# First V in three pieces with the first w_in pieces between them, and four FFN banks filled by head pairs

## The chip, the cores and the metric

The kernel runs on one core of a Trainium2 chip. The metric is device time of one execution in microseconds (us); every run is checked against the reference. A change counts as faster or slower from 2% on. The span that a profile shows is some 1.8 us shorter than the time of the same execution (before: 510.0 against 511.74). Every run quoted here is compared with runs of the same rounds. Some traces lack a few matmul records (before: 2710 matmuls but 2761 weight loads); where one is missing, the view shows a short idle time put down to "issue".

## The reference

Linformer attention, then a squared-ReLU feed-forward network (FFN), all in float32 outside the kernel:

```python
# q, k, v: (8 batches, 8 heads, 1024 tokens, 64);  E, F: (64, 1024)
k_proj = einsum('ks,bhsd->bhkd', E, k);  v_proj = einsum('ks,bhsd->bhkd', F, v)
attn = softmax(q @ k_proj.T / 8)                    # 64 columns
x = (attn @ v_proj) -> (8192 tokens, 512)
out = relu(x @ w_in) ** 2 @ w_out                   # 512 -> 2048 -> 512
```

The FFN is nearly all of the TensorE work. Each later batch's attention is spread among the FFN matmuls of the batch before. The first batch has nothing to hide behind, so the first 25 us or so, the head, are where TensorE can idle. The change is to the head alone.

## The kernel before

The program loads float32 and converts to bfloat16 on the way, on one queue issued by GpSimd (`load`). The loads of the head, in order: K and Q of the first batch by halves, V by halves, then w_in in five pieces and w_out in four:

```python
    for g in range(2):
        load(K0[:, half[g]], tokens(k, 0, h=half[g]))
        load(Q0[:, half[g], 0:4, :], tokens(q, 0, h=half[g], i=slice(0, 4)))
        if g == 0:
            make_identity(nc, ident[:])
            load(f_bf[:], F[:])
    for g in range(2):
        load(V0[:, half[g]], tokens(v, 0, h=half[g]))
```

```python
    W_IN_PIECES = ((0, 2), (2, 4), (4, 8), (8, 12), (12, 16))
    w_in_view = moe_w_in.rearrange("(cb p) f -> p cb f", p=P)
    w_out_view = moe_w_out.rearrange("(fb p) m -> p fb m", p=P)
    w_in_at, w_out_sb = {}, []
    for lo, hi in W_IN_PIECES:
        t = wpool.tile([P, NCB, (hi - lo) * P], BF16, name=f"w_in_{lo}")
        load(t[:], w_in_view[:, :, lo * P:hi * P])
        for fb in range(lo, hi):
            w_in_at[fb] = (t, fb - lo)
    fn = NFB // WP
    for j in range(WP):
        if j == WP - 1:
            load(Q0[:, :, 4:8, :], tokens(q, 0, i=slice(4, 8)))
        t = wpool.tile([P, fn, DM], BF16, name=f"w_out_{j}")
        load(t[:], w_out_view[:, j * fn:(j + 1) * fn, :])
        w_out_sb.append(t)
```

V is projected by F (1024 tokens to 64), half the heads at a time, into both halves of the partitions; `chunk_values` multiplies the exponentials with that and scales the result by the inverse sums into `xT`, the FFN's input. One call covers a group of two head pairs, which are two of xT's four channel blocks:

```python
        def project_v(self, g):

            ps = bank()
            for i in range(NI):
                for o in (LO, HI):
                    nc.tensor.matmul(
                        ps[o, 0:C // 2], lhsT=FT[:, i, :], rhs=V0[:, half[g], i, :],
                        start=(i == 0), stop=(i == NI - 1),
                    )
            nc.vector.tensor_copy(self.vp[:, half[g]], ps[:, 0:C // 2].rearrange("k (h d) -> k h d", d=D))
```

```python
        def chunk_values(self, c, g):
            ps = att_psum()
            e, rs = self.e.pop(g), self.rs.pop(g)
            for j in range(2):
                s = slice(j * HC, (j + 1) * HC)
                self.values_mm(ps[:, :, s], 2 * g + j, e[:, :, s])
            for j in range(2):
                s = slice(j * HC, (j + 1) * HC)
                nc.vector.tensor_tensor(
                    out=self.xT[:, 2 * g + j, c], in0=ps[:, :, s], in1=rs[:, :, s], op=ALU.mult
                )
```

The FFN's first token half starts in two banks of PSUM, the memory that TensorE writes its results to: channel blocks 0 and 1 (head group 0), then 2 and 3 (group 1). Then 14 more banks, then w_out's four pieces in order, for two token blocks at a time:

```python
        def steps(self):
            for c in range(2):
                self.hsq[c] = hsq_pool.tile([P, NFB, TCH], BF16, name="hsq")
                first = self.cold and c == 0
                fb0 = 0
                if first:

                    banks = [bank() for _ in range(2)]
                    for g in range(2):
                        for fb in range(2):
                            for cb in (2 * g, 2 * g + 1):
                                self.first_mm(c, fb, cb, banks[fb])
                            if g == 1:
                                self.square(c, fb, banks[fb])
                        yield
                    fb0 = 2
                for fb in range(fb0, NFB):
                    ps = bank()
                    for cb in range(NCB):
                        self.first_mm(c, fb, cb, ps)
                    self.square(c, fb, ps)
                    yield
                if first:

                    for t0 in range(0, 4, 2):
                        banks = [bank() for _ in range(2)]
                        for j in range(WP):
                            for t in range(2):
                                for fb in range(j * fn, (j + 1) * fn):
                                    self.second_mm(c, t0 + t, fb, banks[t])
                                if j == WP - 1:
                                    self.store(c, t0 + t, banks[t])
                                yield
```

(cut: the ordinary second half.) TensorE's order is written by hand; `warm(n)` issues n matmuls on zeros that only keep the array busy. The end of the head, before the FFN loop:

```python
        att.transpose_k((1,))
        warm(2)
        att.chunk_scores(0, 1)
        warm(2)
        att.project_v(0)
        warm(1)
        att.chunk_sums(0, 1)
        att.chunk_values(0, 0)
        warm(1)
        att.project_v(1)
        att.chunk_values(0, 1)
```

The softmax here doesn't subtract the row's maximum and nothing guards it: scores larger than these inputs give would overflow.

## Time and profile before

| before | |
|---|---|
| time | 512.42 us (511.70 to 512.67, 3 runs) |
| span of the profiled run | 510.0 us |
| TensorE busy | 497.0 us, 97% |
| first V projection begins | 15.98 us |
| FFN reaches the third w_in piece | 25.57 us |
| matmuls of the last w_out piece begin | 42.35 us |

The first extract is TensorE's timeline of the kernel before. Columns: start, duration, engine, line, operation, output<-inputs, shapes, count; in brackets the idle time before it and what ended that.

```profile
15.98 1.06 PE L204 MATMUL ps_bank<-V_sb,FT 128*64 128x256 bf16 x16
17.30 0.41 PE L262 MATMUL ps_att<-expT,ones 64*64 64x512 bf16 x4 [0.25 <-issue]
...
19.74 1.06 PE L204 MATMUL ps_bank<-V_sb,FT 128*64 128x256 bf16 x16 [1.44 <-DMA V_sb<-in_v_dram]
21.32 0.41 PE L266 MATMUL ps_att<-expT,vp 64*64 64x256 bf16 x8 [0.52 <-DVE vp L208]
21.67 1.31 PE L358 MATMUL ps_bank<-xT,w_in_114 128*128 128x512 bf16 x5
23.19 0.81 PE L358 MATMUL ps_bank<-xT,w_in_114 128*128 128x512 bf16 x3 [0.22 <-DVE xT L341]
...
25.57 3.62 PE L358 MATMUL ps_bank<-xT,w_in_118 128*128 128x512 bf16 x16
...
42.35 1.02 PE L364 MATMUL ps_bank<-w_out_131,hsq 128*128 128x512 bf16 x4 [0.19 <-DMA w_out_131<-in_moe_w_out_dram]
```

The reader should see the 1.44 us wait for V's second half, the 0.52 us wait for its cast, and the third w_in piece at 25.57. These are the waits that the change is about. (A busy time ends with the modelled drain of the array; back to back, matmuls of 512 columns follow each other every 0.216 us.)

The second is the chain of waits of the kernel before, in order of time: start, duration, what.

```profile
7.67 14.18 DMA w_in_116<-in_moe_w_in_dram
...
22.14 20.17 DMA w_out_131<-in_moe_w_out_dram
...
42.35 1.04 PE ps_bank L364 x4
```

The chain does not pass through V at all. It runs through the landing of the second w_in piece, which frees a slot in the load queue, and then through the landing of the last w_out piece at 42.31 (issued at 22.14, 20.17 us to landing).

The third is the table of stages of the kernel before: from:to and length, busy time of PE, PEld, DVE, ACT and POOL with counts, granted clock, DMA share, GB/s.

```profile
15.00:20.00 5.00, 3.26 (x45) 1.77 (x48) 1.72 (x3) 3.67 (x4) 0.76 (x2) 1.00 1.33 201
20.00:25.00 5.00, 4.26 (x37) 2.03 (x33) 2.41 (x5) 1.18 (x3) 2.65 (x4) 1.00 1.26 206
25.00:30.00 5.00, 4.95 (x24) 2.26 (x24) 2.43 (x7) 3.48 (x6) 1.69 (x3) 1.00 1.24 206
```

The loads run at a level 201 to 206 GB/s. TensorE is busy 3.26 of 5 us in the stage with the wait for V, and nearly all the time from 25 on.

The last is GpSimd's timeline of the kernel before: its two issues of w_out pieces that were released by the landings of V's two halves.

```profile
16.22 0.74 POOL L76 DMA_DIRECT2D w_out_126<-in_moe_w_out_dram  x1 [1.83 <-DMA V_sb<-in_v_dram]
19.98 0.74 POOL L76 DMA_DIRECT2D w_out_128<-in_moe_w_out_dram  x1 [3.02 <-DMA V_sb<-in_v_dram]
```

The halves, 512 KB each, landed 3.76 us apart in this trace.

### The profile page before, as it was taken

Reading aid. Unit: us, or ns where it says so; the run is one execution under the profiler, and the core shown is the slowest. Engines: PE = TensorE matmul, PEld = TensorE weight load, DVE = VectorE, ACT = ScalarE, POOL = GpSimd, SP = SyncE. Lnnn points to the kernel's source line nnn. Section 1 sums busy time; section 2 is a strip of 40 time slices with the busy share of each in tenths; the row PEclk is TensorE's granted clock in tenths of the full one; section 3 lists DMA queues with packets and bytes.
Section 4 is the critical chain, followed back from the end, with each engine's and each line's share of the span. In section 5 each row is a group of like instructions: output and inputs, shape, how many; then the busy total and the mean of one; then the engine's idle time right before and its main releaser. Section 6 shows DMA issues by size and latency. Waiting matters only on the chain.

```text
span 510.0 us, 6889 instructions
## 1 busy us (share of the span) xinstructions
PE 497.0 (97%) x2710; PEld 222.8 (44%) x2761; DVE 216.7 (42%) x437; ACT 272.4 (53%) x411; POOL 32.0 (6%) x44
## 2 busy tenths in 40 slices
PE   8799999999999999999999999999999999999997
PEld 4344444444444444444444444444444444444444
DVE  2442766444434445235452345444443443522130
ACT  2564484664718556374645736366472755544351
POOL 7320100121000020001000000000000000000000
PEclk9999999999999999999999999999999999999999
DMA  9999999899996199104931060101102011010102
GB/s 156 204 205 222 226 207 202 132 220 207 195 217 125 56 185 201 65 0 126 181 78 42 17 160 1 62 22 42 53 1 82 1 41 42 31 54 21 63 0 82
DMA packets 67840, 53.92 MB, mean 106 GB/s; under 512 B 29152, under 2 KB 59616, under 8 KB 67808
## 3 DMA queue, kind: packets, MB, share of 16 engines
q0 software_dynamic: 30880, 29.49, 36.8%
q1 hardware_dynamic: 36928, 23.99, 17.5%
q8 instruction: 21, 0.34, 0.3%
q14 instruction: 11, 0.09, 0.1%
HBM read 59.24 MB, written 16.78 MB: 149 GB/s over the span
## 4 chain that ended last, share of the span: by engine, by line
PE 88%; DMA 7%; issue 2%; POOL 1%; ACT 1%; DVE 1%; POOLq 0%; ACTq 0%
PE ps_bank L364 41%; PE ps_bank L358 40%; DMA w_out_131<-in_moe_w_out_dram 4%; DMA w_in_116<-in_moe_w_in_dram 3%; PE ps_bank L185 2%; PE ps_att L256 1%; PE ps_att L290 1%; PE ps_att L312 1%; PE ps_bank L312 1%; DVE rs L300 0%; PE ps_bank L241 0%; DVE xT L341 0%; POOL K_sb L76 0%; POOL V_sb L76 0%; ACT expT L270 0%
## 5 line engine op out<-in xcount | busy, mean ns | idle before, releaser
L355 DVE TENSOR_TENSOR hsq<-h_relu 128x512 bf16<-128x512 bf16 x256 | 108.9, 426 | 192.9 <-ACT h_relu L354 192.0
L354 ACT ACTIVATE h_relu<-ps_bank 128x512 bf16<-128x512 f32 x256 | 151.7, 599 | 69.3 <-PE ps_bank L358 69.2
L364 PEld LDWEIGHTS <-hsq 128*128 128x128 bf16 x1040 | 99.5, 98 | 123.6 <-issue 9.3
L371 ACT COPY o_sb<-ps_bank 128x512 f32<-128x512 f32 (+1 forms) x65 | 37.6, 579 | 119.7 <-PE ps_bank L364 110.9
L364 PE MATMUL ps_bank<-w_out_124,hsq 128*128 128x512 bf16 (+1 forms) x257 | 65.6, 376 | 0.2
L364 PE MATMUL ps_bank<-w_out_131,hsq 128*128 128x512 bf16 (+1 forms) x251 | 64.1, 376 | 1.4 <-issue 1.1
L364 PE MATMUL ps_bank<-w_out_128,hsq 128*128 128x512 bf16 (+1 forms) x252 | 64.3, 376 | 1.1 <-issue 1.0
L364 PE MATMUL ps_bank<-w_out_126,hsq 128*128 128x512 bf16 (+1 forms) x249 | 64.2, 376 | 1.1 <-issue 0.8
L300 DVE COPY rs<-rs 32x1024 f32<-32x1024 f32 x60 | 41.3, 689 | 47.2 <-ACT rs L295 45.8
L358 PE MATMUL ps_bank<-xT,w_in_122 128*128 128x512 bf16 x255 | 58.9, 380 | 0.0
L358 PE MATMUL ps_bank<-xT,w_in_118 128*128 128x512 bf16 x250 | 57.7, 380 | 0.4
L358 PE MATMUL ps_bank<-xT,w_in_120 128*128 128x512 bf16 x247 | 57.4, 379 | 0.4
L270 ACT ACTIVATE expT<-ps_att 128x1024 bf16<-128x1024 f32 x32 | 31.8, 1024 | 18.1 <-PE ps_att L256 18.1
L358 PEld LDWEIGHTS <-w_in_120 128*128 128x128 bf16 x256 | 24.9, 98 | 30.4 <-issue 0.4
L358 PEld LDWEIGHTS <-w_in_118 128*128 128x128 bf16 x256 | 24.9, 98 | 30.2 <-issue 0.4
L358 PEld LDWEIGHTS <-w_in_122 128*128 128x128 bf16 x256 | 24.4, 98 | 31.1 <-issue 2.7
L358 PE MATMUL ps_bank<-xT,w_in_114 128*128 128x512 bf16 x128 | 30.6, 379 | 0.3 <-DVE xT L341 0.2
L358 PE MATMUL ps_bank<-xT,w_in_116 128*128 128x512 bf16 x126 | 30.0, 379 | 0.1
L294 ACT ACTIVATE rs<-ps_att 128x1024 f32<-128x1024 f32 x15 | 15.3, 1023 | 12.7 <-PE ps_att L290 12.7
L316 DVE TENSOR_TENSOR xT<-ps_att,rs 128x512 bf16<-128x512 f32 x28 | 18.1, 686 | 8.7 <-PE ps_att L312 8.4
L358 PEld LDWEIGHTS <-w_in_114 128*128 128x128 bf16 x128 | 12.4, 98 | 15.6 <-issue 1.3
L358 PEld LDWEIGHTS <-w_in_116 128*128 128x128 bf16 x128 | 12.5, 98 | 15.2 <-issue 0.2
(71 smaller groups left out, 233.9 us busy)
## 6 DMA issues: line engine op xcount, KB each, us to landing
out_dram<-o_sb SPq DMA_DIRECT2D x63, 256.0 KB, 2.0
K_sb<-in_k_dram POOLq DMA_DIRECT2D x7, 1024.0 KB, 22.1
V_sb<-in_v_dram POOLq DMA_DIRECT2D x7, 1024.0 KB, 26.7
Q_sb<-in_q_dram POOLq DMA_DIRECT2D x7, 1024.0 KB, 15.0
K_sb<-in_k_dram POOLq DMA_DIRECT2D x2, 512.0 KB, 7.1
V_sb<-in_v_dram POOLq DMA_DIRECT2D x2, 512.0 KB, 12.0
Q_sb<-in_q_dram POOLq DMA_DIRECT2D x2, 256.0 KB, 7.6
w_in_118<-in_moe_w_in_dram POOLq DMA_DIRECT2D x1, 512.0 KB, 15.5
```

The costliest lines, as they stand in the source:

```text
L185: nc.tensor.matmul(ps[LO, :], lhsT=ET[:, i, :], rhs=self.K[:, :, i, :], start=f, stop=l)
L256: nc.tensor.matmul(ps[o, par], lhsT=self.kT[r, h % 4, h // 4, :], rhs=self.qT[r, h, n, :], start=True, stop=True)
L270: nc.scalar.activation(e[:], ps[:], AF.Exp, scale=SCALE)
L294: nc.scalar.activation(rs[1][:], ps[:], AF.Ln)
L300: nc.vector.tensor_copy(rs[j][lack:lack + 32], rs[j][have:have + 32])
L312: nc.tensor.matmul(ps_x[par][o], lhsT=self.vp[r, 2 * pr + a, :], rhs=e[r, par], start=True, stop=True)
L316: nc.vector.tensor_tensor(out=self.xT[:, pr, :, par], in0=ps_x[par].rearrange("p (c t) -> p c t", c=2), in1=rs[:, par].rearrange("p (c t) ...
L354: nc.scalar.activation(r[:], ps[:], AF.Relu)
L355: nc.vector.tensor_tensor(out=self.hsq[c][:, fb, :], in0=r[:], in1=r[:], op=ALU.mult)
L358: nc.tensor.matmul(ps[:], lhsT=w_in_blk(cb, fb), rhs=self.xT[:, cb, c].rearrange("p a t -> p (a t)"), start=(cb == 0), stop=(cb == NCB - 1),)
L364: nc.tensor.matmul(ps[:, m], lhsT=self.hsq[c][:, fb, tb * P:(tb + 1) * P], rhs=w_out_blk(fb)[:, m], start=(fb == 0), stop=(fb == NFB - 1),)
L371: nc.scalar.copy(o[:, m], ps[:, m])
```

## The change

The intent: begin the FFN before all of V is there. V comes in pieces of 4, 2 and 2 heads with the first two w_in pieces between them. The FFN starts in four banks instead of two on head group 0, and the last two head pairs of V are projected, multiplied and folded in one after the other while the rest lands.

```diff
--- before.py
+++ after.py
@@ -96,8 +96,8 @@
         if g == 0:
             make_identity(nc, ident[:])
             load(f_bf[:], F[:])
-    for g in range(2):
-        load(V0[:, half[g]], tokens(v, 0, h=half[g]))
+    V_PIECES = (slice(0, 4), slice(4, 6), slice(6, 8))
+    load(V0[:, V_PIECES[0]], tokens(v, 0, h=V_PIECES[0]))
     nc.scalar.preload_act_table_set("natural_log_exp_and_others")
     zeros = const_pool.tile([P, 512], BF16, name="zeros")
     nc.vector.memset(zeros[:], 0.0)
@@ -109,11 +109,13 @@
     w_in_view = moe_w_in.rearrange("(cb p) f -> p cb f", p=P)
     w_out_view = moe_w_out.rearrange("(fb p) m -> p fb m", p=P)
     w_in_at, w_out_sb = {}, []
-    for lo, hi in W_IN_PIECES:
+    for j, (lo, hi) in enumerate(W_IN_PIECES):
         t = wpool.tile([P, NCB, (hi - lo) * P], BF16, name=f"w_in_{lo}")
         load(t[:], w_in_view[:, :, lo * P:hi * P])
         for fb in range(lo, hi):
             w_in_at[fb] = (t, fb - lo)
+        if j < 2:
+            load(V0[:, V_PIECES[j + 1]], tokens(v, 0, h=V_PIECES[j + 1]))
     fn = NFB // WP
     for j in range(WP):
         if j == WP - 1:
@@ -196,16 +198,16 @@
                 )
             self.keep_k(ps[LO, 0:C // 2], g, nc.scalar.copy if g == 0 else None)
 
-        def project_v(self, g):
-
-            ps = bank()
+        def project_v(self, h):
+
+            n = (h.stop - h.start) * D
+            ps = att_psum()[:, 0, 0:n]
             for i in range(NI):
                 for o in (LO, HI):
                     nc.tensor.matmul(
-                        ps[o, 0:C // 2], lhsT=FT[:, i, :], rhs=V0[:, half[g], i, :],
-                        start=(i == 0), stop=(i == NI - 1),
+                        ps[o], lhsT=FT[:, i, :], rhs=V0[:, h, i, :], start=(i == 0), stop=(i == NI - 1)
                     )
-            nc.vector.tensor_copy(self.vp[:, half[g]], ps[:, 0:C // 2].rearrange("k (h d) -> k h d", d=D))
+            nc.vector.tensor_copy(self.vp[:, h], ps.rearrange("k (h d) -> k h d", d=D))
 
         def transpose_k(self, gs=(0, 1)):
             ps = bank([P, H // 2, 2, KP], BF16)
@@ -330,13 +332,13 @@
             self.sums_mm(ps, self.e[g])
             self.rs[g] = self.inverse(ps)
 
-        def chunk_values(self, c, g):
+        def chunk_values(self, c, g, pairs=(0, 1)):
             ps = att_psum()
-            e, rs = self.e.pop(g), self.rs.pop(g)
-            for j in range(2):
+            e, rs = self.e[g], self.rs[g]
+            for j in pairs:
                 s = slice(j * HC, (j + 1) * HC)
                 self.values_mm(ps[:, :, s], 2 * g + j, e[:, :, s])
-            for j in range(2):
+            for j in pairs:
                 s = slice(j * HC, (j + 1) * HC)
                 nc.vector.tensor_tensor(
                     out=self.xT[:, 2 * g + j, c], in0=ps[:, :, s], in1=rs[:, :, s], op=ALU.mult
@@ -379,15 +381,18 @@
                 fb0 = 0
                 if first:
 
-                    banks = [bank() for _ in range(2)]
-                    for g in range(2):
-                        for fb in range(2):
-                            for cb in (2 * g, 2 * g + 1):
+                    banks = [bank() for _ in range(4)]
+                    for cbs, fbs in (
+                        ((0, 1), (0, 1)), ((0, 1), (2, 3)), ((2,), (0, 1)), ((2,), (2, 3)), ((3,), (0, 1, 2, 3)),
+                    ):
+                        for fb in fbs:
+                            for cb in cbs:
                                 self.first_mm(c, fb, cb, banks[fb])
-                            if g == 1:
+                            if cbs[-1] == NCB - 1:
                                 self.square(c, fb, banks[fb])
-                        yield
-                    fb0 = 2
+                        if (cbs, fbs) != ((2,), (2, 3)):
+                            yield
+                    fb0 = 4
                 for fb in range(fb0, NFB):
                     ps = bank()
                     for cb in range(NCB):
@@ -446,13 +451,11 @@
         warm(2)
         att.chunk_scores(0, 1)
         warm(2)
-        att.project_v(0)
+        att.project_v(V_PIECES[0])
         warm(1)
         att.chunk_sums(0, 1)
         att.chunk_values(0, 0)
-        warm(1)
-        att.project_v(1)
-        att.chunk_values(0, 1)
+        warm(2)
 
         coming = None
         for b in range(B):
@@ -462,6 +465,10 @@
                 plan.setdefault(step, []).append(lambda: fn(*args, **kwargs))
 
             if b == 0:
+                at(1, att.project_v, V_PIECES[1])
+                at(2, att.chunk_values, 0, 1, (0,))
+                at(2, att.project_v, V_PIECES[2])
+                at(3, att.chunk_values, 0, 1, (1,))
                 at(21, att.transpose_q_chunk, 1, Q0, 0)
                 at(21, att.transpose_q_chunk, 1, Q0, 1)
                 at(23, att.chunk_scores, 1, 0)
```

On TensorE this is 17 more matmuls (16 narrow projections and one warming); on GpSimd one more load is issued.

## The prediction

> **What bounds the kernel now.** The page gives PE 97% busy at full granted clock in a span of 510.0 us, so only the head of the program has idle TensorE time: in the stage table PE is busy 3.26 of the 5 us from 15 to 20, 4.26 from 20 to 25, and then 4.95 to 5.00. The PE timeline shows the two waits the change aims at: 1.44 us at 18.3-19.7 for the second half of V, and 0.52 us at 20.8-21.3 for the cast of vp, plus 0.22 us for xT; the FFN flows from 23.2 and reaches the third w_in piece at 25.57.
>
> But the chain of waits does not run through these. Its first 43 us are descriptor issues on GpSimd, then the landing of the second w_in piece (issued 7.67, landed 21.85), then that of the last w_out piece (issued 22.14, landed 42.31); PE starts on that piece at 42.35, having waited only 0.19 us. The stage table has the DMA engines at over 1.2 and a level 201 to 207 GB/s from 10 to 43 us. Until 42.3 us the program is DMA-bound: every 512 KB piece lands some 2.55 us after the last (24.4, 26.9, 29.5, 32.0, 34.6, 37.1, 39.8, 42.3), while PE comes to them 1 to 4 us later, except the last one.
>
> **What the change does.** Bytes before the last w_out piece are the same; V's second half is split in two and the two small w_in pieces move between, at the cost of one more issue (0.75 us of GpSimd, mostly waiting anyway). Eight transfers stay in flight: the last w_out piece is now issued when the last V piece lands, instead of the second w_in piece, both at about 21.9. The Trainium skill ("DMA: Bandwidth & Descriptors", "Anatomy of one DMA") says the engines wait on no semaphore but consume their queues; the level GB/s agrees, so reordering does not move the end.
>
> On PE: 16 more narrow projection matmuls and one more warming matmul (about 0.7 us), and sixteen FFN matmuls partly moved forward. My replay with the trace's durations (matmul pitch 0.216, xT 0.69, vp cast about 0.3-0.42): w_in piece one lands about 17.3, V's pieces at about 18.9 and 21.85; the first four FFN matmuls run at 18.8-20.1, the next four at 20.7-21.5; then the last V piece must land, be projected (0.7), cast (0.4), multiplied (0.3) and scaled (0.69), so channel block 3 comes at about 24.3 and PE reaches the third w_in piece at about 25.2 (24.8 to 25.9), against 25.57.
>
> **On the critical path.** PE gains 0.4 us at 25 us and gives all of it back at the last w_out piece, where it will wait about 0.6 us instead of 0.19. After 42.3 both kernels run the same matmuls at 97-99% PE. Net: 0, within run noise (511.7 to 512.67 before) and 0.3 us in that landing.
>
> **Predicted: 512.3 us, 80% range 511.6 to 513.1.** Faster by over 2%: 1%; within 2%: 98%; slower: 1%.
>
> **Right if** the profile shows: the 1.44 us wait for V gone or broken up; third w_in piece begun at 24.8-25.9; last w_out piece landing at 42.3 +- 0.3 and a longer PE wait before it (0.3 to 1 us); from there the same distance to the end as before (467.7 us).
>
> **Wrong if** the last w_out landing moves (microsecond for microsecond); if the last V piece lands later than about 22.5, so that PE falls behind the DMA and reaches the last w_out piece after 42.3; or if the four FFN banks held together stall on their ReLUs (0.6 us each against 0.86 us of matmuls).

## The result, and the profile after

After: 512.57 us median (512.25 to 513.23, 6 runs); before, over the same and earlier rounds: 512.54 us (511.70 to 514.28, 6 runs). The ratio is 0.9997, 95% interval 0.9979 to 1.0014: the same. Ratios are from runs of the same rounds, so not quite the ratio of the medians quoted.

TensorE's timeline of the changed kernel:

```profile
15.70 1.06 PE L207 MATMUL ps_att<-V_sb,FT 128*64 128x256 bf16 x16
...
18.57 0.38 PE L360 MATMUL ps_bank<-xT,w_in_113 128*128 128x512 bf16 x1 [0.34 <-DVE xT L343]
19.17 0.81 PE L360 MATMUL ps_bank<-xT,w_in_113 128*128 128x512 bf16 x3 [0.22 <-DVE xT L343]
19.91 0.64 PE L207 MATMUL ps_att<-V_sb,FT 128*64 128x128 bf16 x16
20.48 1.04 PE L360 MATMUL ps_bank<-xT,w_in_116 128*128 128x512 bf16 x4
...
21.68 0.64 PE L207 MATMUL ps_att<-V_sb,FT 128*64 128x128 bf16 x16
22.61 0.59 PE L360 MATMUL ps_bank<-xT,w_in_113 128*128 128x512 bf16 x2 [0.30 <-DVE xT L343]
23.14 0.30 PE L268 MATMUL ps_att<-expT,vp 64*64 64x256 bf16 x4
23.60 0.38 PE L360 MATMUL ps_bank<-xT,w_in_116 128*128 128x512 bf16 x1 [0.16 <-issue]
24.24 0.59 PE L360 MATMUL ps_bank<-xT,w_in_113 128*128 128x512 bf16 x2 [0.26 <-DVE xT L343]
...
25.30 3.61 PE L360 MATMUL ps_bank<-xT,w_in_119 128*128 128x512 bf16 x16
...
42.05 1.02 PE L366 MATMUL ps_bank<-w_out_132,hsq 128*128 128x512 bf16 x4 [0.16 <-DMA w_out_132<-in_moe_w_out_dram]
```

The 1.44 us wait is gone. In its place stand four short stops for xT (0.22 to 0.34 us) and many short pieces of work. (Two gaps of 0.16 us put down to issue are most likely missing records: at 23.60 the trace has one matmul where the program has two, and in the trace of compute only, where none is missing, both gaps are gone.) The third w_in piece is begun at 25.30 instead of 25.57, but the first V projection had already begun at 15.70 instead of 15.98, before anything of the change could act: from there it is 9.60 us against 9.59. TensorE gained nothing against that trace.

The chain of waits of the changed kernel in the head, and its table of stages:

```profile
8.56 12.97 DMA V_sb<-in_v_dram
...
21.81 20.20 DMA w_out_132<-in_moe_w_out_dram
...
42.05 1.04 PE ps_bank L366 x4
```

```profile
15.00:20.00 5.00, 4.29 (x48) 1.85 (x43) 1.71 (x3) 3.42 (x4) 1.63 (x3) 1.00 1.36 202
20.00:25.00 5.00, 4.28 (x51) 2.18 (x53) 1.87 (x4) 0.35 (x1) 2.89 (x4) 1.00 1.24 206
```

The chain has the same form: the slot is now freed by V's last piece, and the last w_out piece lands at 42.01 (21.81 and 20.20 us after), again 0.3 us ahead like the rest of this trace. TensorE waits 0.16 us for it, as it did 0.19. In these stages the loads run at 202 and 206 GB/s against 201 and 206: their level has not moved.

GpSimd's timeline of the changed kernel, its issues released by V's first and second piece:

```profile
15.94 0.74 POOL L76 DMA_DIRECT2D w_out_125<-in_moe_w_out_dram  x1 [1.80 <-DMA V_sb<-in_v_dram]
19.85 0.74 POOL L76 DMA_DIRECT2D w_out_129<-in_moe_w_out_dram  x1 [1.78 <-DMA V_sb<-in_v_dram]
```

These are 3.91 us apart, so V's second piece came late here too, and TensorE did not wait for it. In the four other traces with this load order and the full loads it is 2.63 to 2.68.

Yet the span is 0.9 us longer. The chain of waits of the changed kernel further on, and what TensorE waited for after 43 us (engine, line, waited for: us in total, times, longest):

```profile
142.86 10.89 DMA out_dram<-o_sb
153.83 0.59 ACT o_sb L373
```

```profile
PE ps_bank L360 <- ACT o_sb L373: 1.2, 1, 1.2
```

The store that the chain runs through took 10.89 us from issue to landing (the median of all of them is 2.1), ScalarE waited for its buffer, and TensorE lost 1.2 us waiting for ScalarE to empty a bank. In the trace of before ScalarE also waited for stores (8.7 us in all), but TensorE did not. Whether that belongs to the change has to be tested.

### The profile page after: what moved, and what is told of

It is laid out like the page before. It is cut to its first block, busy times and chain, and to the rows that moved or that the text cites. A ratio compares the mean times of both kernels' runs of the same rounds, so it can differ in the third digit from the quotient of the medians.

```text
span 510.9 us, 6925 instructions
## 1 busy us (share of the span) xinstructions
PE 497.8 (97%) x2727; PEld 223.2 (44%) x2778; DVE 216.9 (42%) x438; ACT 272.1 (53%) x411; POOL 33.1 (6%) x45
## 4 chain that ended last, share of the span: by engine, by line
PE 85%; DMA 9%; issue 2%; ACT 1%; POOL 1%; DVE 1%; SPq 0%; POOLq 0%; ACTq 0%
PE ps_bank L360 40%; PE ps_bank L366 38%; DMA w_out_132<-in_moe_w_out_dram 4%; DMA V_sb<-in_v_dram 3%; PE ps_bank L187 2%; DMA out_dram<-o_sb 2%; PE ps_att L258 1%; PE ps_att L292 1%; PE ps_att L314 1%; DVE rs L302 1%; PE ps_bank L314 1%; ACT rs L297 0%; ACT rs L296 0%; PE ps_bank L243 0%; DVE xT L343 0%
## 6 DMA issues: line engine op xcount, KB each, us to landing
Q_sb<-in_q_dram POOLq DMA_DIRECT2D x7, 1024.0 KB, 14.6
```

## The experiments

The theories. **Theory 1**: two limits meet at 42 us, TensorE's own chain and the stream of loads, and the change did not shorten TensorE's chain. **Theory 2** (the rival, near to the prediction's wording): TensorE was sped up, and only the landing of the last w_out piece ate it. **Theory 3**: the start of a run varies, and hides or shows the change. **Theory 4**: late output stores add noise of their own.

One measure turned out to be worth more than the times: in each trace, from the first V projection to the first w_out matmul (call it the stretch), and from the start of the second token half's FFN to the end (the tail). Both count on TensorE's timeline.

| trace | first V projection | first w_out matmul | stretch | second half's FFN | span less that |
|---|---|---|---|---|---|
| before | 15.98 | 35.93 | 19.95 | 52.94 | 457.1 |
| after | 15.70 | 35.66 | 19.96 | 52.64 | 458.3 |
| loads only | 17.27 | 37.82 | 20.55 | 54.49 | 457.0 |
| compute only | 17.34 | 37.30 | 19.96 | 53.97 | 457.3 |
| less Q, before | 17.37 | 35.81 | 18.44 | 52.48 | 457.0 |
| less Q, after | 15.70 | 35.69 | 19.99 | 52.35 | 457.0 |
| more warming, before | 16.14 | 34.85 | 18.71 | 53.20 | 458.9 |
| more warming, after | 16.23 | 36.18 | 19.95 | 52.92 | 458.0 |
| warming and six buffers, before | 16.30 | 34.74 | 18.44 | 52.79 | 456.9 |
| warming and six buffers, after | 16.34 | 36.29 | 19.95 | 52.95 | 457.0 |
| six buffers, before | 17.27 | 35.72 | 18.45 | 53.26 | 456.9 |
| six buffers, after | 17.28 | 37.23 | 19.95 | 53.90 | 456.9 |
| last piece later | 18.54 | 36.99 | 18.45 | 53.52 | 456.9 |
| more instructions | 17.07 | 35.51 | 18.44 | 52.90 | 458.6 |

### Loads only

```diff
-    for g in range(2):
-        load(V0[:, half[g]], tokens(v, 0, h=half[g]))
+    V_PIECES = (slice(0, 4), slice(4, 6), slice(6, 8))
+    load(V0[:, V_PIECES[0]], tokens(v, 0, h=V_PIECES[0]))
...
+        if j < 2:
+            load(V0[:, V_PIECES[j + 1]], tokens(v, 0, h=V_PIECES[j + 1]))
```

> The kernel before with the new load order alone (V in pieces of 4, 2 and 2 heads, the small w_in pieces between); its TensorE program is untouched, so the second projection of V needs both later pieces. Theory 1 (two limits meet: TensorE's own chain through the last V piece and the DMA stream both reach the last w_out piece at 42 us): V's last bytes land at about 21.6 instead of 19.7, so the third w_in piece is begun 1.7 us later than before (27.3 instead of 25.6, counted from the same launch) and the whole runs 1.5 to 2 us longer. Theory 2 (only the DMA stream sets the head, TensorE has slack): 0 to 0.3 us.

Measured: 514.66 us (513.22 to 515.98), ratio 1.0046 (1.0026 to 1.0065). TensorE's timeline:

```profile
17.27 1.06 PE L206 MATMUL ps_bank<-V_sb,FT 128*64 128x256 bf16 x16
...
21.63 1.06 PE L206 MATMUL ps_bank<-V_sb,FT 128*64 128x256 bf16 x16 [2.04 <-DMA V_sb<-in_v_dram]
...
37.82 4.48 PE L366 MATMUL ps_bank<-w_out,hsq 128*128 128x512 bf16 x20
```

TensorE waits 2.04 us for V and begins w_out at 37.82. The kernel before with six buffers, whose first V projection began at the same 17.27, begins it at 35.72: the new load order alone costs 2.1 us of the stretch. At the second half's FFN 1.2 us of that are left (54.49 against 53.26). So TensorE has no slack of that size, and the part of theory 2 that has the loads alone decide falls. The medians differ by 2.2 us, but that is not all shown to be the load order: the profiled run, at a mean granted clock of 1.000, is the fastest (513.22), and the other five have 0.997 to 0.992 and are the longer the lower it is (513.93 to 515.98). Why they have it is open.

### Compute only

The changed kernel, with the three V pieces all loaded before w_in:

```diff
-    load(V0[:, V_PIECES[0]], tokens(v, 0, h=V_PIECES[0]))
+    for h in V_PIECES:
+        load(V0[:, h], tokens(v, 0, h=h))
...
-        if j < 2:
-            load(V0[:, V_PIECES[j + 1]], tokens(v, 0, h=V_PIECES[j + 1]))
```

> The changed kernel with its loads put back: all three V pieces before the w_in pieces; TensorE keeps the four banks and the head pairs. Theory 1: the first FFN matmul now waits for the first w_in piece (about 20.3 instead of 18.6), and the third w_in piece is begun at about 26.1, 0.5 to 1 us later than in either kernel; total +0.5 to +1 us. Theory 2: 0. If it is faster than both kernels (third w_in piece before 25), the four banks were a gain of their own that the new load order took away.

Measured: 513.08 us (512.26 to 514.17), ratio 1.0010 (0.9993 to 1.0027). TensorE's timeline:

```profile
17.34 1.06 PE L206 MATMUL ps_att<-V_sb,FT 128*64 128x256 bf16 x16
...
37.30 4.48 PE L365 MATMUL ps_bank<-w_out,hsq 128*128 128x512 bf16 x20
```

The expectation missed in an instructive way. I expected the stretch to grow, because w_in lands later; it is 19.96 us, the same as in the changed kernel. The same TensorE order takes 19.95 to 19.99 us in all six traces that have it, whether V's pieces land early or late. So what holds it is not the landing of V's last piece, as I had thought, but its own order of small dependent steps. (The median rose by 0.6 us, inside the 0.5 to 1 expected, but its interval allows 0, and the trace does not show the reason that was expected.)

### Less Q: the second load of the first Q taken away (wrong result)

```diff
-        if j == WP - 1:
-            load(Q0[:, :, 4:8, :], tokens(q, 0, i=slice(4, 8)))
...
-                        src[:, 4 * hg + hh, 4 * c + 2 * n:4 * c + 2 * n + 2, :]...
+                        src[:, 4 * hg + hh, 2 * n:2 * n + 2, :]...
```

> Wrong result on purpose: the kernel before without the second load of Q for the first batch (512 KB ahead of the last w_out piece; the second token half uses the first half's Q). The last w_out piece then lands about 2.55 us earlier, at 39.8. Theory 1: TensorE was only 0.2 us from that wait, so the last w_out piece is begun only about 0.2 us earlier and the total is 0 to 0.4 us shorter. Theory 2: up to 2.5 us shorter.

> Wrong result on purpose: the changed kernel without the second load of Q for the first batch. This takes the DMA limit away and shows what the change gave TensorE. If it gained 0.4 us at the third w_in piece, as predicted, and only the landing of the last w_out piece ate that, this runs 0.4 us ahead of the same edit of the kernel before (last w_out matmuls begun at 41.5 against 41.9 from the same launch). Theory 1: the change gave TensorE nothing, and the two agree within 0.15 us in the trace.

Measured, before: 511.15 us (509.98 to 511.23), ratio 0.9967 (0.9952 to 0.9983). After: 512.36 us (511.12 to 512.61), ratio 0.9989 (0.9972 to 1.0005). Both outputs agreed with the reference within its tolerance, which here says little.

The kernel before gained 1.3 us where theory 1 gave it 0 to 0.4, so the load stream held it up more than its trace showed. The changed kernel gained hardly anything. With this limit gone the changed kernel is 1.1 us slower than the kernel before (means 512.01 and 510.92, standard error 0.34), where theory 1 expected the two to agree: the change does not merely give TensorE nothing, it costs it time, and theory 2, with a gain hidden by the landing, falls here. The traces say why: the kernel before took 18.44 us for the stretch here, not 19.95. Its first V projection began late (17.37), V's second half was there when TensorE came to it, and there was no wait for it at all. The 19.95 of the trace of before was the odd one, not the rule.

### More warming, and six output buffers

In the traces with the eight warming matmuls unchanged, the four that follow at 5.9 us took either 1.04 us or 1.89 us, and the first V projection began at 15.7 to 16.0 or at 17.3 to 17.4 accordingly (once 18.5). The Trainium skill, "TensorE: Matmul & The Clock Gate" ("Part 1: The HAM clock gate"), says that the array starts at half rate and is let go by a free-running window of about 3.4 us, so that the moment differs from run to run. The traces agree that it differs, but by far more than the ±500 ns that the page gives: full rate from 4 to 5 us, from about 10, or once from about 12.

```diff
-        warm(8)
+        warm(11)
```

> The kernel before with 11 warming matmuls in place of 8 at the start, so that TensorE has no gap of 0.44 us before the first transposes. In three of the six traces so far TensorE ran at half rate until about 10 us (four warming matmuls took 1.89 us instead of 1.04) and reached the first V projection at 17.3 instead of 15.8. Theory 3 (the start decides run by run, and the kernel before hides a late start in its 1.44 us wait for V): full rate by 7 us in the trace, first V projection at 16.2 or earlier, and the total moves by less than 0.3 us.

> The changed kernel with the same 11 warming matmuls. It has no long wait left in which to hide a late start, so by theory 3 a late start costs it about 1.3 us and this edit takes the slow half of its runs away: median down by 0.3 to 1 us against the changed kernel's 512.57, and runs closer together than its own 511.1 to 512.6 without the second Q load. Rival: the start doesn't matter and the median stays within 0.2 us of 512.5.

And with it six buffers for the output instead of four:

```diff
-    out_pool = ctx.enter_context(tc.tile_pool(name="outp", bufs=4))
+    out_pool = ctx.enter_context(tc.tile_pool(name="outp", bufs=6))
```

> As the previous edit of the kernel before, and six output buffers instead of four. Theory 4 (output stores that land late hold up the copy out of PSUM and, in some runs, TensorE): waits of ScalarE for output stores (8.7 us in the trace of before) gone or under 3 us; median 0.3 to 1 us below the same kernel with four buffers. Rival: nothing changes, since TensorE did not wait in that trace.

> As the previous edit of the changed kernel, and six output buffers instead of four. Theory 4: the 1.2 us that TensorE lost at 153 us to a store in the trace of after is gone and the median falls by 0.5 to 1.2 us. Against the same edits of the kernel before: within 0.3 us (theory 1), or 0.4 us faster if the change has a gain of its own that noise had hidden.

Measured: more warming, before 513.01 us (512.45 to 513.86), ratio 1.0011 (0.9997 to 1.0024), after 513.44 us (512.62 to 514.76), ratio 1.0022 (1.0006 to 1.0038). With six buffers too, before 511.47 us (511.00 to 511.59, 5 runs), ratio 0.9978 (0.9965 to 0.9990), after 511.81 us (511.59 to 513.49), ratio 0.9993 (0.9977 to 1.0009).

The warming did what it should in all four traces (full rate by about 7.2 us) and did not help: both medians rose (by 0.5 and 0.9 us), where theory 3 had expected the one unmoved and the other lower. In that form theory 3 falls; what is left of it is that starts differ and that the kernel before takes up part of a late one: with six buffers (the traces of this section and the next) a start 0.97 us later brought it to the second half's FFN only 0.47 us later (53.26 against 52.79), and the changed kernel 0.95 us later for 0.94 (53.90 against 52.95). With four buffers TensorE lost time to late stores again; this is the kernel before with more warming, after 43 us:

```profile
PE ps_bank L358 <- ACT o_sb L371: 1.6, 2, 0.9
```

With six buffers no wait for a store is left, the tails are 456.9 and 457.0 us, and the medians fell by more than 1.5 us. Theory 4 holds for the traces: the tail is 456.9 to 457.1 us wherever TensorE did not wait for a store, with either kernel, and longer only where it did. The 1.2 us of the trace of after is this kind of loss, and not the change alone: the kernel before loses 1.6 us in the same way here.

The pair with six buffers shows the change best, because both versions began alike. TensorE's timeline, before and after:

```profile
16.30 1.06 PE L204 MATMUL ps_bank<-V_sb,FT 128*64 128x256 bf16 x16
...
34.74 4.48 PE L364 MATMUL ps_bank<-w_out,hsq 128*128 128x512 bf16 x20
39.66 1.07 PE L231 MATMUL ps_bank<-ident,Q_sb 128*128 128x128 bf16 x16 [0.44 <-DMA Q_sb<-in_q_dram]
...
42.20 1.02 PE L364 MATMUL ps_bank<-w_out,hsq 128*128 128x512 bf16 x4 [0.61 <-DMA w_out<-in_moe_w_out_dram]
43.15 0.63 PE L256 MATMUL ps_att<-qT,kT 64*64 64x256 bf16 x16
```

```profile
16.34 1.06 PE L207 MATMUL ps_att<-V_sb,FT 128*64 128x256 bf16 x16
...
36.29 4.48 PE L366 MATMUL ps_bank<-w_out,hsq 128*128 128x512 bf16 x20
40.60 1.06 PE L233 MATMUL ps_bank<-ident,Q_sb 128*128 128x128 bf16 x16
41.50 1.89 PE L366 MATMUL ps_bank<-w_out,hsq 128*128 128x512 bf16 x8
43.32 0.63 PE L258 MATMUL ps_att<-qT,kT 64*64 64x256 bf16 x16
```

The kernel before is at w_out 1.55 us earlier (34.74 against 36.29) and then waits 0.44 us for Q's second half and 0.61 us for the last w_out piece. The changed kernel comes later and waits for neither. At the scores that follow, only 0.17 us of the 1.55 are left (43.15 against 43.32). This is how a TensorE order that is 1.5 us longer can cost almost nothing.

### Six output buffers alone

The edit is the second one above, by itself.

> The kernel before with six output buffers instead of four and nothing else. If stores that land late cost TensorE time in most runs, the median falls by 0.7 to 1.3 us, to about 511.4, and no wait of ScalarE for an output store is left in the trace. If the gain of the earlier pair came from the longer warming, nothing changes.

> The changed kernel with six output buffers. With the store waits gone on both sides the change itself is left: 0.2 to 0.6 us slower than the same edit of the kernel before if the change only lengthens TensorE's head (the earlier pair with more warming gave 0.34), equal within 0.1 if both are held by the last w_out piece, faster if the change has a gain of its own.

Measured: before 511.61 us (511.18 to 511.97), ratio 0.9983 (0.9962 to 1.0003); after 512.43 us (511.24 to 513.87), ratio 0.9998 (0.9975 to 1.0021). No wait for a store is left in either trace. They began at 17.27 and 17.28, and the stretches are again 18.45 and 19.95. With this later start the kernel before waits only for the last w_out piece (0.61 us), and 0.64 us of the 1.5 are left at the second half's FFN (53.26 against 53.90). The kernel before gained 0.56 us in the medians, a little less than the 0.7 to 1.3 expected, and the change costs 0.8 us, more than the 0.2 to 0.6 expected.

In the three pairs (more warming, both, six buffers alone) the mean of the changed kernel's runs lies 0.56, 0.73 and 0.78 us above that of its partner, on average 0.69 with a standard error of 0.21 worked out from the spread of the runs (0.56 when the cores' spans are compared instead of the times). Unedited, the two kernels showed no difference, but the interval there, up to 1.0014, allows 0.7 us. That the change costs a little, about 0.1%, is likely; it is far inside "the same".

GpSimd's timeline of the kernel before with six buffers, the same two issues as shown of before:

```profile
16.68 0.74 POOL L76 DMA_DIRECT2D w_out<-in_moe_w_out_dram  x1 [1.81 <-DMA V_sb<-in_v_dram]
19.23 0.74 POOL L76 DMA_DIRECT2D w_out<-in_moe_w_out_dram  x1 [1.80 <-DMA V_sb<-in_v_dram]
```

Here V's halves landed 2.55 us apart. In six of the seven traces with V in halves it is 2.53 to 2.61; only in the trace of before is it 3.76. With V in pieces, the second piece was late in the trace of after (3.91) and in that of less Q (4.07). So in three of the fourteen traces a transfer of V was late by more than 1 us. In the one of the kernel before the stretch is 1.5 us longer (19.95 against 18.44), in the two of the changed order it is not (19.96 and 19.99 against 19.95): that is what the change buys. It is also why the first two traces, both with a late V, looked equal in the head.

### The last w_out piece later

Six buffers, and the last w_out piece's sixteen matmuls behind the others of all four token blocks, so that TensorE need not wait for it (the transposes of Q's second half one step later, in PSUM space of the attention):

```diff
-                    for t0 in range(0, 4, 2):
-                        banks = [bank() for _ in range(2)]
-                        for j in range(WP):
-                            for t in range(2):
+                    banks = []
+                    for ts, js in (((0, 1), (0, 1, 2)), ((2, 3), (0, 1, 2)), ((0, 1, 2, 3), (3,))):
+                        if js[0] == 0:
+                            banks += [bank() for _ in ts]
+                        for j in js:
+                            for t in ts:
...
-                at(21, att.transpose_q_chunk, 1, Q0, 0)
+                at(22, att.transpose_q_chunk, 1, Q0, 0)
```

> The kernel before with six output buffers, and the sixteen matmuls of the last w_out piece put behind those that need only the first three pieces, for all four token blocks; the transposes of Q's second half are one step later. If the wait for Q and the last w_out piece (1.05 us together in the trace of the kernel with more warming and six buffers) is what holds TensorE, it is gone and the total falls by 0.5 to 1.2 us against six buffers alone, to 510.2 to 511; if the softmax chain of the second token half then holds the FFN, the gain is under 0.3 us and TensorE waits for xT at about 51 us instead.

Measured: 512.09 us (511.14 to 512.87), ratio 0.9990 (0.9968 to 1.0013). Inconclusive. In the trace the waits for Q and w_out are gone and none for xT came in their place, but this profile fell on the latest start of all (first V projection at 18.54), so that they might have been gone anyway. It reached the second half's FFN only 0.26 us after the kernel with six buffers alone, although it began 1.27 us later. The median, however, is 0.5 us above six buffers alone and not below. Why is open.

### More TensorE instructions

What made V's second half late in the trace of before? In each of the first ten traces one instruction block of 16 KB was moved by a DMA engine between 17.4 and 19.1 us. The Trainium skill, "Runtime: NRT & Kernel Launch" ("Instruction fetch mechanics"), says that programs are fetched in blocks of 16 KiB, 256 instructions. Each time TensorE stood at about its 250th instruction, matmuls and weight loads counted together. So the start of TensorE's program was padded: the eight warming matmuls were cut into 68 narrow ones.

```diff
-        warm(8)
+        ps = bank()
+        for j in range(68):
+            nc.tensor.matmul(ps[0:D, 0:D], lhsT=zeros[:, 0:D], rhs=zeros[:, 0:D], start=True, stop=True)
```

> The kernel before with its 8 warming matmuls of 512 columns cut into 68 of 64 columns: about the same TensorE time, 120 more TensorE instructions. In all ten traces so far a transfer of one 16 KB instruction block takes 0.9 to 1.0 us on one DMA engine, between 17.4 and 19.1 us, each time when TensorE is at about its 248th instruction. If it is TensorE's program being fetched, it now comes when TensorE is at its second K projection, at 12 to 13.7 us, and V's second half lands at 18.2 to 18.6, not at 19.7 as in the trace of before. If the block has nothing to do with TensorE's count, it stays at 17.4 to 19.1.

Measured: 513.29 us (513.05 to 514.14, 4 runs), ratio 1.0019 (0.9989 to 1.0049); its trace lost 1.2 us of TensorE time to late stores. The DMA view of 1 us of the kernel before (17 to 18) and of this one (11 to 12): queue, kind, packets, MB, share of 16 engines in that window.

```profile
q8 instruction: 1, 0.02, 5.6%
```

```profile
q8 instruction: 1, 0.02, 5.9%
```

5.6% of 16 engines for 1 us is 0.90 us of one engine; 5.9% is 0.94. The block moved with TensorE's instruction count, from 17 to 11 us: it is TensorE's program. In this trace the second half of K, in flight at 11 to 12, was the one that came late: TensorE waited for it until 13.25, against 11.86 to 12.11 in the traces of after and before. (In two other traces K's second half came as late, but after a late first half.) That fits a block holding up whatever one engine has queued behind it. V's second half came 2.53 us after the first, as in most traces, though later than the 18.2 to 18.6 expected, since the first was later too. For V in the trace of before this is not shown: in two edited traces of the kernel before (more warming, without and with six buffers) the block came at 17.65 and 17.95, and V was not late. In the two traces of the changed kernel with a late V it came at 17.45 and 17.65. What decides which transfer is hit is open.

## Why the prediction was right, and where it was not

- **The time**: 512.57 against 512.3 predicted, in the range 511.6 to 513.1. Right, but in part by luck: the predicted sum is a gain of 0.4 us on TensorE less a wait that eats it. Neither term was there; in its place the changed order loses 1.5 us of TensorE time where V is on time, mostly hidden by waits that the kernel before has and the changed one has not.
- **The stream of loads keeps its end.** Predicted 42.3 within 0.3 for the last w_out landing; 42.01 in the trace, at the same GB/s. Right; in the three edited pairs with the full loads (more warming, both, six buffers alone) the landing of the changed kernel lies between 0.3 us before and 0.4 us after that of its partner. The skill's statement quoted in the prediction, that DMA engines wait on no semaphore, is in keeping with that, and no run contradicts it.
- **"PE gains 0.4 us at 25 us."** Wrong. Raw it was 0.27 us, all of it from an earlier start of the run: from the first V projection it is 9.60 us against 9.59. And measured against the kernel before with V on time, TensorE lost 1.5 us (stretch 19.95 against 18.44). Two things failed in this step. The replay put the third w_in piece 9.2 us after the first V projection (25.2 less 15.98), and it took 9.60; that it was begun at 25.30, near the 25.2, is owed to the earlier start. And the comparison took the 1.44 us wait for V in one trace for the rule: it appeared in only one of the seven traces with V in halves; one other had 0.19 us, the rest none.
- **"It will wait about 0.6 us instead of 0.19"** for the last w_out piece. Wrong, the other way round: it is the kernel before that waits 0.56 to 0.61 us there in its four edited traces that keep the full loads and w_out's order, and the changed kernel that waits 0.16 us or not at all. What the landing hides is a loss of the change, not a gain.
- **"From there the same distance to the end (467.7 us)."** It was 468.9 in the profiled run; 1.2 us of that is the wait for an output store, which the kernel before has in other traces too (1.6 us with more warming). Nothing shows it to be a part of the change.
- **Where the 1.5 us come from.** In the kernel before, the projection of V's second half, about 1 us of useful work, stands between the values of the first head group and the FFN, and covers the scaling into xT. In the changed order the FFN follows at once and TensorE waits for xT four times (1.1 us in all), with two warming matmuls as filling. The sum, as an estimate from two traces that lack no record (less Q, before, and compute only): 0.4 us more waits (1.1 against 0.7); 0.3 us for one more warming matmul; 0.15 us for sixteen more projection matmuls of half the width (0.57 us a group against 1.0); and 0.6 us because the 64 FFN matmuls of w_in come in six groups instead of two and take 14.6 us instead of 14.0 (a lone one is shown at 0.38 us, where in a row each takes 0.216).

The causes shown: the TensorE order costs 1.5 us of the stretch whatever the order of loads (compute only); the order of loads alone costs 2.1 us of it (loads only, one trace); together they cost no more than the TensorE order alone; and what the kernel before loses at its waits for Q's second half and for the last w_out piece (waits of 1.05 us with an early start, 0.61 with a late one) hides most of that: 0.16 and 0.64 us are left at the second half's FFN. How the 1.5 us divide is an estimate and was not tested term by term.

## What to carry to other kernels

A wait in one trace is not yet a wait in most runs: look at what it stood on (a landing, a start) in a second trace before building a change on its removal. An order that makes a rare late landing harmless can cost more in the usual run, as here. The work that an order moves may have been covering something; ask what useful work stood there to hide the next dependency, and what will hide it afterwards. When two limits end together, here TensorE's order and the last load, a change to one of them shows only after the other is moved, and a loss in it can be as invisible as a gain. The change worth keeping is outside the subject: six output buffers instead of four took the late-store waits away (511.61 us alone, 511.47 with more warming), although 0.2% is close to what the runs can tell.

## What the Trainium skill lacked or had wrong

- "Runtime: NRT & Kernel Launch" ("Instruction fetch mechanics") calls the cost of crossing a 16 KiB boundary mostly hidden. The size agrees (16 KB), and so does the count (the block came when TensorE was at about its 250th instruction, and moved with the count). What it lacks: the block takes 0.90 to 0.98 us of one of the DMA engines that carry the data, and so may come in the way of loads there (K's second half 1.1 to 1.4 us later in the trace with more instructions than in those of before and after; one trace, and other traces have the block with no transfer late).
- "DMA: Bandwidth & Descriptors" ("Issuing engines are not separate DMA queues") says that transfers of all issuing engines interleave on the same 16 DMA engines. The runs agree and give a size that the page lacks: an output store of 256 KB took 10.89 us from issue to landing while loads were moving too, against a median of 2.1. That the loads were the reason was not tested.
- "TensorE: Matmul & The Clock Gate" ("Part 1: The HAM clock gate") says that the release differs from run to run, by ±500 ns; the traces have a wider spread (four warming matmuls in 1.04 or 1.89 us, full rate from 4 to 5, about 10 or about 12 us). No page says that the profile's granted-clock column does not show it: it reads 1.00 in the first stages of the traces of both kernels, while TensorE's first warming matmuls run at about half rate (eight of them in 3.59 and 3.28 us; in a row at full rate one takes 0.216).
